# A new order for the operations and loads of an attention and feed-forward kernel on one core

## The chip, the core and the metric

The kernel runs on one core of a Trainium2 chip. The metric is the device time in microseconds (us), from the start of an execution to its end. Three executions of the kernel before took 324.38, 324.75 and 325.0 us; the median is 324.75.

## What is computed

Attention over 8 batches of 8 heads, then a feed-forward layer on its output. Each head has 576 tokens of 64 values. Ahead of the keys and values stand 16 "beacon" keys and values that every token sees; among the rest a token sees itself and what comes before it.

```python
def _attn_ref(q, k, v, beacon_k, beacon_v):      # q, k, v: [8, 8, 576, 64]; beacons: [8, 8, 16, 64]
    k_all = np.concatenate([beacon_k, k], axis=2)
    v_all = np.concatenate([beacon_v, v], axis=2)
    scores = scale * np.matmul(q, k_all.transpose(0, 1, 3, 2))          # scale = 1 / 8
    causal[:, Nb:] = np.triu(np.ones((S, S), dtype=bool), k=1)
    scores = np.where(causal, -1000000000.0, scores)
    a = np.exp(scores - scores.max(-1, keepdims=True))
    a /= a.sum(-1, keepdims=True) + 1e-09
    return np.matmul(a, v_all)

def _moe_ref(x, w_in, w_out):                    # x: [4608, 512], w_in: [512, 2048], w_out: [2048, 512]
    r = np.maximum(x @ w_in, 0.0)
    return (r * r) @ w_out
```

Inputs and output are float32; the kernel works on bfloat16 copies and accumulates in float32.

## The kernel before, in words

**An order written out.** The kernel first makes a list of operations, each with a name, the engines that may do it, the operations it needs, and what it takes and gives of the shared PSUM banks. Nothing is emitted at that point. Then `Order.run` (from line 202) walks the string SEQUENCE (lines 17 to 167), word by word, and emits each named operation. A suffix picks the engine where there is a choice: `@A` is ScalarE (ACT), `@D` VectorE (DVE), `@P` GpSimd (POOL); without one the first engine of the operation's list is taken. Two lines show how the banks are handed out:

```python
op.slots[pool] = [self.pools[pool].pop(0) for _ in range(need)]
...
self.pools[pool].append(from_op.slots[pool][which])
```

A bank is taken from the front of a queue and given back at its end, in the order of the words. So the order of SEQUENCE decides three things: the order in which every engine works through its own instructions (each engine is in order and runs beside the others, held only by what its operations need), the place of each load in the queue of the engine that issues it, and which earlier operation an operation waits for when it takes a bank. PSUM has four banks "ps" for most products, two double strips for scores, and there are three SBUF buffers "held". Words such as `fillg3` or `tpg0.0.1k` emit nothing; they only give a bank back.

**Fillers.** `fill0` to `fill59` (L354) are 60 matmuls on a tile of ones that write a bank nobody reads. They stand among the first operations, where TensorE (PE) has little else to do.

**Attention.** Pairs of heads are numbered 0 to 31, four for each batch. In a name the first number is the pair (for `qk`, `exp`, `mask`, `av`, `norm`) or the batch (for loads and transposes).

- *First loads of batch 0* (L550): `fldk0`, `fldk1`, `fldk2` go through SyncE's queue (SP), `fldq0` to `fldq2` through ACT's; they bring the first 240 tokens of pair 0, of pair 1, and of pairs 2 and 3. `fck` and `fcq` (L372 on ACT, L374 on DVE) cast them to bfloat16. `bkl` and `bkc` load and cast the beacon keys.
- *Other loads of batches 0 and 1*: `sld...` (L472) and `ld...` (L408 queries, L416 and L417 keys, values and beacon values) go through POOL's queue, and so do the weights, `win0` to `win3` (L893) and `wout0` to `wout3` (L902), a quarter each.
- *Transposes*: for batches 0 and 1 on PE, `tp` (L487 for the first 240 tokens of batch 0, L489 else), with evictions `ek` and `eq` (L372, L374). From batch 2 on `tr` is a transposing DMA on SP.
- *Scores* `qk` (L649) fill a strip. Batch 0 is split in a small first part (240 tokens) and three larger pieces; later batches run as a stream of pieces. `exp` (L671 for batch 0, L747 after) takes the exponential on ACT. `mask` zeroes what a token may not see, on POOL (affine select, L776) or on DVE (a minimum with the tile `tri`, L780). `tri` itself (L343, L345) and `ident` are made on POOL.
- *Values* `av` (L802) multiply with the values and a column of ones; `norm` (L819, L821, DVE) divides by the sum that this column gives.
- *Transposed x* for the feed-forward part: batches 0 to 2 on PE (`xtp` L870, copied by `xte`, L372 or L374), later batches by transposing DMAs on SP (`xt`, L853). A batch's `xt` needs all eight of its norms.

**Feed-forward.** The tokens are cut in nine chunks of 512. `s1.j...` is the first product of chunk j: plain for chunks 0 to 2 (L1088, four matmuls for each block of 128 features; chunk 0 in two parts, so the last number is 0 or 1), and for chunks 3 to 8 a scheme that saves an eighth of the multiplications: seven products for each of four units (L985), as `s1.6.3.4` is product 4 of unit 3 of chunk 6. It needs differences of the tokens, `xsum` (L961, DVE or POOL), and of the weights, `asum` (L928). The partial results pass through `h` operations: `c1`, `u2`, `u3` copy a bank to a held buffer (L372 or L374), `c11`, `c22`, `c12` add a held buffer and apply the relu (L1023, DVE), `c21` is a relu alone (L1014, L1016). `relu` (L1102, L1104) and `sq` (L1049, L1051, L1112, L1114) finish the plain chunks and the squares. `s2.j...` is the second product: chunk 0 plain (L1137), the others with the same scheme (L1194), which needs sums of the activations, `sum` (L1163, DVE or POOL), and of the weights, `wsum` (L913). `ev` (L1217, L372, L374) collects the result, and `st` stores it through SP (L1125; the last chunk in pieces, L1251, one of them through ACT's queue). `warm` (L566) is an exponential on a small tile that nothing reads.

**What orders the work.** Chunk j's first product needs the transposed x of its tokens, so the attention of a batch runs beside the feed-forward products of the chunks before it, and PE takes them in turns. The order around each place that the prediction speaks of is thus that of SEQUENCE alone.

## Time and profile before

| | |
|---|---|
| three executions | 324.38, 324.75, 325.0 us; median 324.75 |
| the profiled execution | 325.59 us |
| its span (first to last instruction) | 323.9 us |
| granted TensorE clock, mean | 0.999 |
| busy: PE, DVE, ACT, POOL | 97%, 78%, 66%, 60% of the span |

The profile is of one execution. Times in it are us from the start of the span. A row of the timeline reads: start, duration of the group, engine, line, operation, the tiles written and read, shapes, the number of instructions, and in brackets the idle time ahead of it with what ended it ("[0.87 <-DVE g L1023]": 0.87 us idle until a DVE instruction of line 1023 was done). A group "x4" is four like instructions in a row, and its duration goes from the first one's start to the last one's end. The table by stretches gives for each stretch the sum of busy time of PE, the weight loads (PEld), DVE, ACT and POOL with their instruction counts, then the granted clock, the mean DMA share and GB/s. The view of waits gives for a kind of wait the us in all, the number, and the longest. In the costliest groups "17.3, 381" is 17.3 us in all and 381 ns for one, and behind the second bar stands the idle time ahead of them.

### The profile page before, as it was taken

To read this page: it belongs to the slowest core of one execution; us is meant where nothing else is said; L and a number is where in the kernel's file an instruction comes from. 1 tells how busy PE (TensorE), PEld (TensorE's weight loads), DVE (VectorE), ACT (ScalarE), POOL (GpSimd) and SP (SyncE) were. 2 spreads that over 40 slices of the span, in tenths; PEclk is the share of its full clock that TensorE was granted. 3 is DMA by queue.
4 is the path that set the end of the run, shared out by engine and by line. 5 is a ranking of instruction groups with operands and counts; after the bars stand their busy time and mean duration, and the time that the engine had idled before them with its cause. 6 is when DMAs were issued, how large, how long until landed. Compare 5 with 4: busy or idle time off the path is not lost.

```text
span 323.9 us, 9406 instructions
## 1 busy us (share of the span) xinstructions
PE 313.9 (97%) x3882; PEld 247.4 (76%) x3882; DVE 252.1 (78%) x529; ACT 213.1 (66%) x313; POOL 195.8 (60%) x268
## 2 busy tenths in 40 slices
PE   7899999999999999998999999999999989999995
PEld 5569765644886468887788888888898878888884
DVE  2687698758976798789997998896867987695773
ACT  2785588257677794768657996889767545555720
POOL 8574679496189588888293759956606051535340
PEclk9999999999999999999999999999999999999999
DMA  8999999999999999999799969944523430110043
GB/s 162 178 179 200 189 182 114 146 199 178 146 78 157 198 174 84 124 222 155 61 130 135 212 68 128 149 88 142 49 16 91 110 52 0 68 65 2 0 148 113
DMA packets 153188, 39.60 MB, mean 122 GB/s; under 512 B 140730, under 2 KB 148794, under 8 KB 153146
## 3 DMA queue, kind: packets, MB, share of 16 engines
q0 software_dynamic: 103744, 18.10, 71.7%
q1 hardware_dynamic: 48253, 20.29, 30.3%
q10 hardware_dynamic: 1149, 0.62, 0.7%
q8 instruction: 30, 0.49, 0.6%
q14 instruction: 12, 0.10, 0.1%
HBM read 37.22 MB, written 9.44 MB: 144 GB/s over the span
## 4 chain that ended last, share of the span: by engine, by line
PE 89%; DVE 3%; DMA 3%; ACT 2%; issue 1%; POOL 0%; DVEq 0%; POOLq 0%; ACTq 0%
PE ps L1194 28%; PE ps L985 21%; PE ps L1088 13%; PE ps L802 9%; PE strip L649 6%; PE ps L1137 4%; DMA qk_area<-in_k_dram 3%; PE ps L649 2%; PE strip L1194 2%; DVE g L1023 1%; PE ps L870 1%; PE ps L354 1%; ACT pt L747 1%; PE ps L489 1%; PE ps L487 1%
## 5 line engine op out<-in xcount | busy, mean ns | idle before, releaser
L1194 PEld LDWEIGHTS <-g 128*128 128x128 bf16 x768 | 72.7, 98 | 10.8 <-issue 1.4
L747 ACT ACTIVATE pt<-strip 128x1024 bf16<-128x1024 f32 x70 | 70.2, 1032 | 5.7 <-PE strip L649 5.7
L1023 DVE CUSTOM_DVE_ANT_0 g<-ps,spare 128x512 bf16<-128x512 f32 x72 | 48.8, 686 | 17.9 <-PE ps L985 12.1
L1194 PE MATMUL ps<-w_out,g 128*128 128x256 bf16 x480 | 60.9, 273 | 0.0
L776 POOL TENSOR_SCALAR_AFFINE_SELECT pt<-pt 128x256 bf16<-128x256 bf16 (+1 forms) x80 | 33.3, 437 | 27.9 <-ACT pt L747 23.9
L372 ACT COPY spare<-ps 128x512 f32<-128x512 f32 x54 | 31.5, 588 | 25.9 <-PE ps L985 21.7
L1163 POOL TENSOR_TENSOR g<-g 128x1024 bf16<-128x1024 bf16 x13 | 28.0, 2158 | 31.5 <-DVE g L1163 10.8
L408 POOL DMA_DIRECT2D qk_area<-in_q_dram x48 | 35.2, 742 | 17.3 <-DMA qT<-qk_area 14.3
L985 PEld LDWEIGHTS <-w_in 128*128 128x128 bf16 x480 | 39.3, 96 | 7.6 <-issue 2.7
L1088 PE MATMUL ps<-xT,w_in 128*128 128x512 bf16 (+2 forms) x256 | 44.1, 326 | 0.0
L985 PE MATMUL ps<-xT,w_in 128*128 128x256 bf16 (+4 forms) x384 | 42.7, 247 | 0.3 <-DMA xT<-xn 0.2
L802 PE MATMUL ps<-vb,pt 128*128 128x65 bf16 (+1 forms) x960 | 38.5, 194 | 1.8 <-DVE g L1023 0.9
L802 PEld LDWEIGHTS <-pt 128*128 128x128 bf16 (+1 forms) x960 | 35.6, 97 | 5.9 <-issue 2.6
L417 POOL DMA_DIRECT2D vb<-in_v_dram x40 | 34.4, 860 | 6.2 <-DMA qk_area<-in_q_dram 2.3
L1088 PEld LDWEIGHTS <-w_in 128*128 128x128 bf16 x256 | 24.0, 98 | 16.3 <-issue 1.0
L1049 ACT ACTIVATE g<-g 128x1024 bf16<-128x1024 bf16 x31 | 32.2, 1058 | 5.6 <-DVE g L1023 4.1
L821 DVE TENSOR_TENSOR xn<-ps,rcp 128x320 bf16<-128x320 f32 (+2 forms) x64 | 31.5, 492 | 2.2
L985 PEld LDWEIGHTS <-qk_area 128*128 128x128 bf16 x320 | 27.8, 97 | 5.2 <-issue 0.8
L747 ACT ACTIVATE pt<-ps 128x512 bf16<-128x512 f32 x42 | 23.6, 598 | 9.6 <-PE ps L649 8.8
L1194 PE MATMUL ps<-w_sum,g 128*128 128x256 bf16 x224 | 28.9, 273 | 0.0
L985 PE MATMUL ps<-spare,qk_area 128*128 128x256 bf16 x192 | 27.9, 272 | 0.5 <-DVE spare L961 0.5
L649 PEld LDWEIGHTS <-kT 64*128 64x128 bf16 x618 | 19.8, 94 | 10.7 <-issue 7.8
(87 smaller groups left out, 492.0 us busy)
## 6 DMA issues: line engine op xcount, KB each, us to landing
out_dram<-osb SPq DMA_DIRECT2D x16, 512.0 KB, 3.8
qk_area<-in_q_dram POOLq DMA_DIRECT2D x48, 72.0 KB, 4.8
vb<-in_v_dram POOLq DMA_DIRECT2D x24, 128.0 KB, 6.0
qk_area<-in_k_dram POOLq DMA_DIRECT2D x18, 128.0 KB, 4.7
w_in<-in_moe_w_in_dram POOLq DMA_DIRECT2D x4, 512.0 KB, 9.4
w_out<-in_moe_w_out_dram POOLq DMA_DIRECT2D x4, 512.0 KB, 9.2
vb<-in_v_dram POOLq DMA_DIRECT2D x8, 112.0 KB, 5.2
qk_area<-in_k_dram POOLq DMA_DIRECT2D x6, 112.0 KB, 4.5
```

Of the source, the lines that this page charges most:

```text
L372: nc.scalar.copy(dst, src)
L408: return [nc.gpsimd.dma_start(out=qb[:, g, :, D * u:D * u + D], in_=t[b, c].rearrange("(n p) d -> p n d", p=NP))]
L417: insts.append(nc.gpsimd.dma_start(out=dst[lo:rows], in_=t[b, :, t0:t0 + rows - lo, :].transpose([1, 0, 2])))
L649: nc.tensor.matmul(out, kc[b % 2][hp, c, pr] if b >= NPE else kT[b % 2][hp, pr, 128 * c:128 * c + 128], rhs, start=True, stop=True)
L747: nc.scalar.activation(out, in_, AF.Exp, bias=0.0, scale=scale)
L776: nc.gpsimd.affine_select(out=d[:, :, i], in_=d[:, :, i], compare_op=ALU.is_ge, fill=0.0, base=Nb if m0 + i == 0 else 0, pattern=[[0, 2], ...
L802: nc.tensor.matmul(a[:, at + (t - tl[0]) * (D + 1):at + (t - tl[0] + 1) * (D + 1)], P[0:rr, hj, o:o + 128], vb[b % 2][0:rr, c, 2 * pr + hj ...
L985: nc.tensor.matmul(o[:, i * HT + at:i * HT + at + w], lhs[:, m, f * 128:(f + 1) * 128], part[:, m], start=fresh and i == 0 and at == 0 and ...
L1023: nc.vector._custom_dve(TENSOR_ADD_SAT, out=dst, in0=bank_of(chain), in1=held[keep[added].held[1]].rearrange("p (f t) -> p f t", f=2), s0= ...
L1049: nc.scalar.activation(both, both, AF.Square, bias=0.0, scale=1.0)
L1088: nc.tensor.matmul(h[:, lo - spans[0][0]:hi - spans[0][0]], w_in_sb[:, mc, ft * 128:(ft + 1) * 128], xT[:, mc, lo % RING:lo % RING + hi - lo],
L1194: nc.tensor.matmul(o, lhs[:, f, t * 128:(t + 1) * 128], rhs[:, f], start=fresh and f == 0, stop=f == HF - 1, skip_group_check=True)
```

## The change

Only the string SEQUENCE is changed. The same words stand in it, 1737 before and after, so the same operations are emitted; their order is another, and so is the engine of some that have a choice. Taking the engine moves together: 27 masks go from DVE to POOL and 32 from POOL to DVE; of relus 16 go from ACT to DVE and 14 the other way, of squares 12 and 14; five sums and three `xsum` go from POOL to DVE and four sums from DVE to POOL.

- *Start.* SP issues `fldk2`, `fldk1`, `bkl0`, `fldk0`, `bkl1` where it issued `fldk0`, `fldk1`, `bkl0`, `fldk2`, `bkl1`. ACT issues `fldq1` ahead of `fldq0`. POOL makes `tri` ahead of its first load, and its queue then holds `win1`, `win2`, `win0`, `win3` where it held `win0`, `win2`, `win1`, `win3`, with the loads of values and of batches 1 and 2 between them in another order. 43 fillers stand ahead of the first score product `qk0.0.0` and 17 behind it, where it was 39 and 21. The first products `s1.0.6.0`, `s1.0.5.0` and others stand ahead of `qk2.1.1`, `av0.1.0`, `av1.1.0` and more steps of batch 0 that they stood behind.
- *Middle.* Masks, evictions and products change places with near neighbours all along, and PE's order comes back to the same set of done products every few steps. Around `av18.0.0` and `av19.0.0` the value steps are spread between other products, `mask19.0.1.1` goes to POOL, and the bank that `av18.0.0` takes is the one `h3.2.c21` gives back, where it was that of `h3.2.c12`.
- *Towards the end.* `av30.0.1` with its norms comes ahead of `av31.0.0`; the four `xsum7` stand together ahead of `sum6.3.1`; `s1.7.1.1` stands ahead of `s1.7.0.4`; `warm` is the last word.

The whole string is rewritten; these are the lines of the start, of the two inner places, and of the end, first as they were and then as they are.

```diff
--- before.py
+++ after.py
@@ -15,155 +15,156 @@
 
 
 SEQUENCE = """
...
-fillg10 fill36 fillg36 fillg56 fill46 fillg46 fill39 fill31 fillg31 fldk0 ident fldk1 bkl0 fck1 fck0 bkc0 tp0.0.0k
-fillg39 ek0.0.0@D fill29 fillg29 fill9 fillg9 fill49 fillg49 fill21 fillg21 tpg0.0.0k fill28 fill51 fillg51 fillg28
-tpb0 fill8 fillg8 ekb0 sld0k1.0 tri fldq0 fldq1 ld0v1 sld0q1.0 ld0v0 fldq2 fcq1 fcq0 tp0.0.0q fill26 fillg26 eq0.0.0@A
-fill17 fillg17 tpg0.0.0q tp0.0.1k fill52 fillg52 tp0.0.1q fill38 fillg38 ek0.0.1@D eq0.0.1@A tp0.1.0k tp0.1.1k
-ek0.1.0@A ek0.1.1@D fcq2@D tpg0.0.1k tpg0.0.1q tpg0.1.1k fldk2 fck3 fcq3@A qk0.0.0 qk1.0.0 fill41 fillg41 tpg0.1.0k
-tp0.0.3q fill6 fill54 fillg6 fillg54 fill18 fillg18 tp0.0.3k fill14 fill5 eq0.0.3@D tpg0.0.3q fillg14 fillg5 tp0.1.0q
-tp0.1.1q tp0.0.2q exp0.0.0 exp1.0.0 eq0.1.0@A ek0.0.3@D eq0.0.2@A qk3.0.0 qk0.1.0 mask0.0.0@D eq0.1.1@D fck2
-mask1.0.0@D tpg0.0.2q tpg0.1.0q tpg0.0.3k fill13 tpg0.1.1q fillg13 fill4 av0.0.0 fillg4 bkl1 exp3.0.0 fill44 fill12
-tp0.0.2k qk1.1.0 fillg12 fillg44 sld0k1.2 sld0q1.2 ld0v3 ld0v2 win0 ld0v4 mask3.0.0@P win2 exp0.1.0 fill0 fill30
-norm0.0.0 av1.0.0 ek0.0.2@D fillg30 tpg0.0.2k fillg0 norm1.0.0 exp1.1.0 qk1.1.2 av3.0.0 tp0.1.2k xtp0.0.0 xte0.0.0@D
-norm3.0.0 qk2.0.0 exp1.1.2 exp2.0.0 ek0.1.2@D fill1 tp0.1.2q qk0.1.2 mask2.0.0@D eq0.1.2@D fillg1 fill53 fill37
-fillg37 fillg53 tpg0.1.2k qk0.1.1 fill16 fillg16 fill3 fillg3 av2.0.0 fill50 fill24 fillg24 tpg0.1.2q exp0.1.2
-exp0.1.1 qk1.1.1 fillg50 win1 mask1.1.1@P norm2.0.0 xtp0.0.3 tp0.1.3k xte0.0.3@D qk2.1.1 ek0.1.3@D exp1.1.1
-mask0.1.1@P win3 sld1k0.0 sld1q0.0 sld1k0.2 mask1.1.0@D xtp0.0.2 fill15 fillg15 tpg0.1.3k tp0.1.3q fill20 fillg20
...
-s1.3.3.2 h3.3.c11 s1.3.2.7 s1.3.3.6 sq3.1.0@A h3.2.u3@A s1.3.2.5 av17.0.1 h3.3.u2@D h3.2.c22 exp19.13.1.0.0 norm17.0.1
-s1.3.3.7 s1.3.2.4 s1.3.2.3 h3.3.u3@A s1.3.3.5 s1.3.3.4 mask19.0.1.1@D mask19.0.2@D h3.2.c12 exp19.13.0.0.0 h3.2.c21@A
-h3.3.c22 mask19.0.1.0@D h3.3.c21@A sq3.2.0@A sq3.3.1@A mask18.0.1.1@P mask19.0.0.0@P mask19.0.0.1@P mask18.0.2@P ld6q4
-mask18.0.0.1@P ld6q5 ld6q6 mask18.0.1.0@P ld6q2 ld5v2 qk20.2 av18.0.0 sq3.2.1@D norm18.0.0 s1.3.3.3 h3.3.c12 av19.0.0
-av18.0.1 av19.0.1 s2.3.2.0 sq3.3.0@A norm18.0.1 norm19.0.1 sum3.1.0@P s2.3.1.0 sum3.1.1@D s2.3.5.0 s2.3.1.1 norm19.0.0
...
-mask31.0.0.0@P mask31.0.0.1@P mask31.0.1.1@P av30.0.0 norm30.0.0 s1.6.3.7 av31.0.0 s1.6.3.5 h6.3.u3@A sq6.2.1@A
-s1.6.3.4 av31.0.1 norm31.0.0 h6.3.c22 h6.3.c21@A sq6.3.1@A sq6.2.0@A av30.0.1 norm31.0.1 norm30.0.1 s1.6.3.3 s1.6.3.2
-s2.6.2.0 s2.6.2.1 st11 xt6.3 xt6.4 st10 xt6.2 xt7.0 h6.3.c12 h6.3.c11 sq6.3.0@D sum6.1.1@D xsum7.1@D xsum7.2@D
-s2.6.1.0 s1.7.0.1 s1.7.1.1 h7.0.c1@A s1.7.0.6 h7.0.u2@A s2.6.1.1 sum6.3.1@D xsum7.3@D xsum7.4@D s1.7.0.7 h7.0.u3@A
-s1.7.0.4 ev6.c1.None@A sum6.2.0@D sum6.2.1@D s2.6.6.0 h7.0.c21@A ev6.c11.None s1.7.0.5 sum6.4.0@P sum6.4.1@P h7.0.c22
...
+fillg55 fill15 fill54 fillg54 fillg15 fill29 fill35 fillg35 fill14 fillg14 fillg29 fldk2 fill13 fill43 fillg43 fillg13
+fill5 fill57 fillg57 fill16 fillg5 fill1 fillg16 fillg1 fill53 fillg53 fldk1 fck1 tp0.0.1k fill20 fillg20 fill36
+fillg36 fill44 fillg44 bkl0 bkc0 fck3 ek0.0.1@D tpb0 fill34 tpg0.0.1k fillg34 fldk0 ekb0 fck0 fldq1 fldq0 fldq2 fcq3@D
+fcq0 fcq1 tp0.0.0q fill10 fillg10 fill39 fillg39 fill17 eq0.0.0@A tp0.0.1q fillg17 tpg0.0.0q tp0.0.0k fill8 fillg8
+sld0k1.0 sld0q1.0 sld0k1.2 ld0v1 ld0v0 sld0q1.2 win1 ek0.0.0@D fcq2@D fck2 eq0.0.1@A tp0.1.1k tp0.1.0k ek0.1.0@D
+tpg0.0.1q tp0.0.3k ek0.0.3@A ek0.1.1@A tpg0.0.3k tpg0.1.0k tpg0.0.0k qk0.0.0 qk1.0.0 tp0.0.3q eq0.0.3@D fill3 tp0.1.0q
+fillg3 tpg0.1.1k fill22 tp0.1.1q eq0.1.0@D exp0.0.0 exp1.0.0 eq0.1.1@D qk3.0.0 bkl1 exp3.0.0 tpg0.1.0q fillg22
+tpg0.0.3q tp0.0.2k fill49 tp0.0.2q mask1.0.0@D fillg49 tpg0.1.1q qk1.1.0 fill4 fill28 ek0.0.2@D eq0.0.2@D fillg28
+tpg0.0.2q tpg0.0.2k fillg4 qk0.1.0 ld0v2 win2 mask0.0.0@P mask3.0.0@P ld0v3 ld0v4 av1.0.0 exp1.1.0 exp0.1.0 av0.0.0
+qk1.1.2 fill59 fillg59 norm1.0.0 win0 norm0.0.0 av3.0.0 fill7 fill6 fillg7 fillg6 qk2.0.0 norm3.0.0 exp1.1.2 exp2.0.0
+fill26 xtp0.0.0 fillg26 tp0.1.2k xtp0.0.1 xte0.0.0@D tp0.1.3q eq0.1.3@A qk0.1.2 tpg0.1.3q exp0.1.2 xte0.0.1@D
+mask2.0.0@D qk0.1.1 fill31 fill19 fillg31 fillg19 ek0.1.2@D av2.0.0 fill21 tpg0.1.2k fill41 fillg21 fillg41 fill58
+fill0 fillg0 fillg58 tp0.1.2q fill33 fillg33 tp0.1.3k norm2.0.0 xtp0.0.2 xtp0.0.3 eq0.1.2@D xte0.0.3@D exp0.1.1
+ek0.1.3@D win3 qk1.1.1 xte0.0.2@A qk2.1.0 exp2.1.0 exp1.1.1 tpg0.1.3k tpg0.1.2q ld2q1 zero2 mask0.1.0@P sld1k0.0 ld2k0
+ld2q4 sld1q0.0 sld1k0.2 wout0 ld1v0 sld1q0.2 ld2q7 ld2k4 wout1 ld2q6 ld2q5 wout2 wout3 ld1v4 s1.0.6.0 s1.0.5.0 bkc1
+tpb1 ekb1 mask0.1.1@D relu0.6.0@D qk2.1.1 s1.0.7.0 exp2.1.1 relu0.7.0@D s1.0.9.0 s1.0.10.0 qk3.1.0 qk2.1.2 mask2.1.1@D
+relu0.5.0@D relu0.10.0@D mask1.1.1@D mask1.1.0@D s1.0.11.0 av0.1.0 norm0.1.0 mask2.1.0@D av1.1.0 relu0.9.0@A exp2.1.2
+exp3.1.0 norm1.1.0 relu0.11.0@A qk3.1.1 exp3.1.1 mask3.1.0@D qk3.1.2 exp3.1.2 s1.0.0.0 s1.0.1.0 s1.0.3.0 av2.1.0
...
+norm17.0.1 s1.3.2.4 h3.2.c21@A h3.2.c22 sq3.1.1@D sq3.2.1@D s1.3.3.7 h3.3.u3@A s1.3.3.5 s1.3.2.3 h3.2.c12 h3.3.c22
+exp19.13.0.0.0 mask19.0.0.0@P mask19.0.0.1@P mask18.0.2@P mask18.0.1.0@P ld6q2 mask18.0.1.1@P ld6q3 ld6q5 ld6q1 ld6q6
+av18.0.0 mask19.0.1.1@P mask19.0.2@D mask19.0.1.0@D s1.3.3.4 h3.3.c21@A sq3.3.1@A qk20.2 av18.0.1 s1.3.3.3 av19.0.0
+norm18.0.0 ld6q7 ld6k4 sum3.1.0@P h3.3.c12 norm19.0.0 norm18.0.1 s2.3.2.0 av19.0.1 sq3.2.0@A s2.3.2.1 norm19.0.1 xt4.2
+xt4.1 xt4.0 sq3.3.0@A s2.3.1.0 s2.3.1.1 exp20.2.1.0.0 ev3.c1.None@A exp20.2.0.0.0 sum3.1.1@D sum3.3.1@D sum3.3.0@D
...
+mask30.0.1.1@P mask30.0.1.0@P mask31.0.0.0@P mask31.0.1.0@P mask31.0.0.1@P sum6.3.0@P av30.0.0 s1.6.3.7 av30.0.1
+norm30.0.0 norm30.0.1 s1.6.3.5 sq6.2.1@A av31.0.0 h6.3.u3@A s1.6.3.4 h6.3.c22 h6.3.c21@A sq6.3.1@A sq6.2.0@A av31.0.1
+norm31.0.0 s1.6.3.2 s1.6.3.3 norm31.0.1 s2.6.2.0 s2.6.2.1 st11 st10 xt6.2 xt6.4 xt7.0 h6.3.c11 h6.3.c12 sq6.3.0@D
+sum6.1.1@D xsum7.1@D xsum7.2@D xsum7.3@D xsum7.4@D sum6.3.1@D s1.7.0.1 s2.6.1.0 h7.0.c1@A s1.7.0.6 h7.0.u2@A s2.6.1.1
+s1.7.0.7 h7.0.u3@A s1.7.1.1 s1.7.0.4 ev6.c1.None@A sum6.2.0@D sum6.2.1@D s2.6.6.0 ev6.c11.None h7.0.c21@A s1.7.0.5
...
+st8.0.0.256 st8.1.1.0 s2.8.3.1 ev8.c12.1 st8.0.1.256 warm
 """
 
 
```

## Prediction

> **What bounds the kernel now.** The page comes first: its span, the busy share of TensorE (PE), and the chain of work that ended last.

> ```profile
> span 323.9 us, 9406 instructions
> PE 313.9 (97%) x3882; PEld 247.4 (76%) x3882; DVE 252.1 (78%) x529; ACT 213.1 (66%) x313; POOL 195.8 (60%) x268
> PE 89%; DVE 3%; DMA 3%; ACT 2%; issue 1%; POOL 0%; DVEq 0%; POOLq 0%; ACTq 0%
> ```

> The reader is to see that PE is the bound: 89% of the chain is matmuls. The change leaves every matmul in place, so only PE's empty time and its fillers can change. The table by stretches shows where that is (after the engines' busy times: PE clock, DMA share, GB/s).

> ```profile
> 0.00:5.00 5.00, 3.19 (x16) 2.26 (x17) 1.20 (x8) 1.78 (x3) 4.04 (x12) 1.00 0.53 131
> 5.00:10.00 5.00, 3.81 (x37) 2.93 (x35) 1.42 (x4) 0.93 (x3) 3.68 (x6) 1.00 1.65 198
> 10.00:15.00 5.00, 4.96 (x75) 3.29 (x76) 3.81 (x12) 4.38 (x9) 3.08 (x5) 1.00 1.74 175
> 140.00:160.00 20.00, 18.33 (x290) 15.82 (x288) 18.73 (x38) 16.20 (x23) 13.86 (x20) 1.00 1.47 142
> 250.00:265.00 15.00, 13.66 (x190) 11.83 (x189) 13.40 (x27) 8.16 (x12) 4.04 (x6) 1.00 0.44 91
> ```

> Two inner stretches lose PE time: 1.67 us in 140 to 160 and 1.34 us in 250 to 265, both with DVE at about 90%. The clock is 1.00 everywhere, so it explains nothing. The third place is the start, where "busy" deceives: the 60 fillers count as busy.

> The view of waits, PE's rows, puts a size on each:

> ```profile
> PE ps L487 <- DMA qk_area<-in_k_dram: 1.2, 1, 1.2
> PE ps L802 <- DVE g L1023: 0.9, 1, 0.9
> PE ps L985 <- ACT spare L372: 0.7, 1, 0.7
> PE ps L802 <- DVE pt L780: 0.5, 1, 0.5
> PE ps L985 <- DVE spare L961: 0.5, 1, 0.5
> PE ps L802 <- DVE xn L821: 0.3, 1, 0.3
> PE ps L985 <- DMA xT<-xn: 0.2, 1, 0.2
> ```

> All waits behind the start add to 3.1 us, about 1% of the span. That is nearly the whole prize.

> **Part 1, the first loads.** Operations are found in the trace by counting: an engine runs its instructions in the order of SEQUENCE.

> ```profile
> 2.23 0.42 SPq L550 DMA_DIRECT2D osb<-in_k_dram  x1
> 4.26 0.50 DVE L374 CAST qk_area<-osb 120x256 bf16<-120x256 f32 x2 [2.51 <-DMA osb<-in_k_dram]
> 6.96 0.41 DVE L374 CAST kT<-ps 128x240 bf16<-128x240 f32 x1 [0.30 <-PE ps L487]
> 10.04 0.49 PE L487 MATMUL ps<-ident,qk_area 112*64 112x112 bf16 x12 [1.24 <-DMA qk_area<-in_k_dram]
> 10.46 0.87 PE L649 MATMUL strip<-qT,kT 64*128 64x240 bf16 x8
> 11.07 1.46 ACT L671 ACTIVATE pt<-strip 128x736 bf16<-128x736 f32 x2
> 13.44 3.13 ACT L671 ACTIVATE pt<-strip 128x736 bf16<-128x736 f32 x4
> 16.77 1.73 ACT L671 ACTIVATE pt<-strip 128x736 bf16<-128x736 f32 x2 [0.20 <-PE strip L649]
> osb<-in_k_dram SPq DMA_DIRECT2D x1, 240.0 KB, 7.9
> ```

> SP's queue ends with fldk2, issued at 2.23 and landed 7.9 later, at 10.1. The new order sends fldk2 first and fldk0 last. The bytes ahead of the last landing stay the same, so I put fldk0 at about 10.1. Behind it stand a cast (0.50 for two, so 0.25), tp0.0.0k (some 0.2, as twelve transposes take 0.49), and ek0.0.0 with 0.41. The first score product then starts at 10.1 + 0.25 + 0.2 + 0.41 and an estimated 0.2 of hand-overs, 11.2 where it was 10.46: 0.7 late. On POOL tri also goes ahead of the first load, which puts sld0k1.0 back by the length of tri, under 1 us; what needs it comes behind what needs fldk0, so it adds nothing while it lands before 11.

> ACT makes that up. Between 11.07 and 16.77 it runs six exponentials (1.46 + 3.13 = 4.6) with two copies and some waiting between them; the new order puts those copies, eq0.1.0 and eq0.0.2, on DVE. Starting 0.7 later, at 11.8, the six end at 16.4, and with up to 0.4 of waiting exp2.0.0 starts between 16.4 and 16.8. So ACT's chain is level again.

> What is left is PE's filling in between. Behind the first score the old order has 21 fillers, the new one 17, since the first feed-forward products (s1.0.6 and so on) move ahead of five score and value steps, with win1 loaded first instead of third.

> ```profile
> L893 POOL DMA_DIRECT2D w_in<-in_moe_w_in_dram x4: 747/758/771, 11.2 to 17.1; - x4
> DMA to landing us min/median/max: 8.1/9.4/11.1
> 23.11 0.58 PE L1088 MATMUL ps<-xT,w_in 128*128 128x240 bf16 x4
> 1.81 5.01 PE L354 MATMUL ps<-ones 128*128 128x256 bf16 x28 [1.81 <-DVE ones L348]
> ```

> A filler has 256 columns. 28 of them took 5.0 us at the start, 0.18 each; eight products of that width take 1.07 in the row at 258.32 below, 0.13 each, and I take that one, as the nearer in time to full flow. Four fewer give 0.5 us. The last of the four loads is issued at 17.1 and lands 11.1 later, at 28.2, in both orders, and they are some 2.6 apart, so win0, third in the new order, lands near 25.6. PE comes to s1.0.0 at about 25.4, an estimate from the products ahead of it. That cover is thin: 0.1 to 0.4 us of wait there. **I take -0.3 us**; the ends are +0.8 (the late first score is not made up) and -2.3 (most fillers become work: 21 x 0.13 = 2.7, less 0.4 for win0).

> **Part 2, 150 to 158.**

> ```profile
> 153.72 0.61 PE L802 MATMUL ps<-vb,pt 128*128 128x65 bf16 x15 [0.87 <-DVE g L1023]
> 155.58 0.94 PE L802 MATMUL ps<-vb,pt 128*128 128x65 bf16 x25 [0.48 <-DVE pt L780]
> 156.81 0.62 PE L802 MATMUL ps<-vb,pt 128*128 128x65 bf16 x15 [0.29 <-DVE xn L821]
> 151.01 2.06 DVE L780 TENSOR_TENSOR pt<-pt,tri 128x256 bf16<-128x256 bf16 x2
> 154.19 1.33 DVE L780 TENSOR_TENSOR pt<-pt,tri 128x256 bf16<-128x256 bf16 x1
> 153.21 2.15 POOL L1163 TENSOR_TENSOR s_sum<-g 128x1024 bf16<-128x1024 bf16 x1
> L780 DVE TENSOR_TENSOR pt<-pt,tri 128x256 bf16<-128x256 bf16 x47 | 17.3, 381 | 1.3 <-ACT pt L747 1.2
> ```

> av18.0.0 waits for the PSUM bank that h3.2.c12 gives back on DVE, and that stands behind mask19.0.1.1, the row at 151.01: two masks in 2.06 where the mean is 0.38. The second long mask ends just behind POOL's sum, 155.5 against 155.4. In the new order av18.0.0 gets its bank from h3.2.c21 on ACT, mask19.0.1.1 goes to POOL, and the four value steps are spread between s1.3.3.4, qk20.2, s1.3.3.3 and s2.3.2.0. mask19.0.1.0 stays on DVE, but av19.0.0, which reads it, comes two products later. The three waits are 1.64; **I take -1.3**, with 0 as the end at which mask19.0.1.0 is as late again, and -1.7, all that the stretch lost.

> **Part 3, 255 to 263.**

> ```profile
> 255.80 6.50 SPq L853 DMA_TRANSPOSE xT<-xn  x5
> 255.28 0.49 DVE L821 TENSOR_TENSOR xn<-ps,rcp 128x320 bf16<-128x320 f32 x1
> 258.32 1.07 PE L985 MATMUL ps<-xT,w_in 128*128 128x256 bf16 x8 [0.18 <-DMA xT<-xn]
> 259.87 0.61 PE L985 MATMUL ps<-spare,qk_area 128*128 128x256 bf16 x4 [0.48 <-DVE spare L961]
> 262.48 0.60 PE L985 MATMUL ps<-spare,w_in 128*128 128x256 bf16 x4 [0.67 <-ACT spare L372]
> ```

> xt7.0, the first of the five transposes, starts when the last of eight normalizations ends: 255.28 + 0.49 = 255.8. That last one (norm30.0.1) stood behind norm31.0.1 and h6.3.c22; the new order does av30.0.1 before both av31, so one normalization less is left at the end, some 0.4 sooner. xsum7.1 and xsum7.2 follow it, with sum6.3.1 moved behind all four, and s1.7.1.1 now stands in the slot before s1.7.0.4. The waits are 1.33. **I take -0.7**; ends 0 and -1.4.

> **Part 4, everything else.** In the rest the PE order returns to the same place every few products; 32 masks go from POOL to DVE and 27 the other way, and activations, copies and squares change sides in like numbers. Five more masks are 5 x 0.38 = 1.9 us on DVE, hidden where DVE has room (252 of 324) and not in the two stretches above. The reordered later loads hide behind PE: its only DMA wait there is the 0.2. If that cover is gone, masks queue behind a load that POOL holds back, at up to a mask's wait each.

> What this trace can't show is where the new order stalls. The nearest row is the collision above, 0.87 of PE's time. **I take one of them, +0.9**; ends 0 and +3.0, as many as all of the old waits.

> **Sum.** -0.3 - 1.3 - 0.7 + 0.9 = -1.4. The profiled execution took 325.59 (span 323.9 and 1.7 around), so one like it would take 324.2. The median of the runs shown is 0.84 lower, 324.75, so 324.75 - 1.4 = 323.35, **323.4 us**.

> **Rivals.** *Collisions (slower).* The mechanism is a mask on DVE that runs beside POOL and takes 1.33, or 2.06 for two, where the mean of 47 is 0.38. For it speak the two rows above; against it that masks move both ways in nearly equal numbers. If the gain of parts 2 and 3 is spent on such waits and two more hit PE, the sum is -0.3 + 2 x 0.87 = +1.4, **326.1**. It decides the sign from the fourth collision that PE waits for (-2.3 + 4 x 0.87 = +1.2); three cancel the gain. [...]

> *The stalls only move (no change).* PE's in-order queue fills each gap in one place and opens it in another; the late k0 (+0.7 passed through) and win0 (+0.4) eat what parts 2 and 3 give. Part 1 is then +1.1: 1.1 - 1.3 - 0.7 + 0.9 = 0.0, **324.8**. It needs fldk0 to land past 10.8, or ACT to wait between the first exponentials.

> **Chances.** Forecast 0.50, its own range 321.4 to 324.0; collisions 0.32; stalls only moved 0.18. Some 0.2%, 0.65 us, is about what a measurement of this kernel can tell from no change. So faster 0.50, same 0.18, slower 0.32. The low end takes two thirds of what the far ends of parts 1 and 3 would add to the forecast (2.0 + 0.7 = 2.7), 323.35 - 1.9 = 321.4; the high end is the collisions with one more of 0.87, 327.0.

> **What will show it.** Part 1: first score near 11.2, exp2.0.0 near 16.8, the first L1088 product some 3 us before 23.1, the longest PE wait of the inner start on win0. Part 2: no PE wait for L1023 or L780 near 153. Part 3: xt7.0 near 255.0 less the gains before it, and waits on L961 and ACT's copies under 0.7 together. Part 4: PE's waits behind the start add to less than 2. I am wrong if the first exponentials start past 12.3, or the L780 mean rises past 0.45 us with PE waiting for it.

## The result, and the profile after

The new order is slower. Four executions took 329.46 to 330.4 us, median 329.88, where the kernel before took 324.88 in four; the ratio is 1.0146, with a 95% interval of 1.0122 to 1.0170. The forecast was 323.4, and 321.4 to 327.0. The profiled execution took 329.70 us, its span 328.0, so 4.1 more than the span before.

First the page of the new kernel: the span, the engines' busy time, and the chain that ended last. Every line number is one higher than before, because the string is one line longer.

```profile
span 328.0 us, 9371 instructions
PE 314.9 (96%) x3872; PEld 248.0 (76%) x3882; DVE 255.1 (78%) x536; ACT 214.4 (65%) x317; POOL 185.8 (57%) x258
PE 88%; DVE 9%; issue 1%; ACT 1%; ACTq 0%; DVEq 0%
```

PE is busy 1.0 us longer with the same matmuls (ten of their records are missing in this trace), and DVE's share of the chain went from 3% to 9%. Both are signs to follow: PE waits for DVE, and PE itself is slow somewhere. PE's longest waits behind the start in the new kernel (us in all, number, longest):

```profile
PE ps L803 <- DVE pt L781: 2.9, 2, 2.7
PE ps L986 <- DVE g L1024: 1.8, 2, 1.4
PE ps L803 <- DVE xn L822: 0.5, 1, 0.5
PE ps L986 <- DMA xT<-xn: 0.4, 1, 0.4
PE ps L986 <- ACT g L1015: 0.2, 1, 0.2
PE ps L986 <- ACT spare L373: 0.2, 1, 0.2
PE ps L986 <- DVE spare L962: 0.2, 1, 0.2
```

Behind the start no wait was over 0.9; now there are a 2.7 and a 1.4. The waits of the old order for L1023 (0.9) and L780 (0.5) at 153 are gone, as forecast. The table by stretches of the new kernel (sums of busy time of PE, PEld, DVE, ACT, POOL; then clock, DMA share, GB/s), with a stretch of its own behind the long wait:

```profile
140.00:160.00 20.00, 19.64 (x307) 17.22 (x305) 18.60 (x40) 16.17 (x24) 12.71 (x19) 1.00 1.31 152
190.00:194.00 4.00, 4.00 (x52) 3.09 (x52) 3.83 (x11) 0.20 (x2) 0.00 (x0) 0.57 0.11 22
```

140 to 160 lost 1.67 us before and 0.36 now. From 190 to 194 PE counts as busy without a gap, but the granted clock is 0.57: this is the second sign. PE did about half the work there in the same time: the first eight products of L1195 in it take 1.90 us, and the same eight take 1.04 in e6 below, at a clock of 1.00. The column of busy time can't show it.

To find where the 4.1 us come from, take places at which both orders have done the same set of products, and compare when the next one starts. New minus old:

| same work done up to (old start) | new - old, us | change |
|---|---|---|
| 45.2 | -0.99 | start: -0.99 |
| 64.6 | -0.19 | **55 to 61: +0.80** |
| 149.9 | -0.20 | |
| 156.8 | -1.68 | 150 to 157: -1.48 |
| 188.4 | -1.74 | |
| 191.8 | +2.36 | **187 to 194: +4.10** |
| 225.1 | +2.20 | |
| 262.5 | +2.08 | 250 to 264: -0.1 |
| 286.4 | +2.23 | |
| 291.0 | +3.64 | **288 to 294: +1.41** |
| end of the span | +4.1 | tail: +0.4 |

So the change gave 2.6 us and took 6.7. The rows of DVE at the three bad places in the new kernel:

```profile
56.83 1.22 DVE L781 TENSOR_TENSOR pt<-pt,tri 128x256 bf16<-128x256 bf16 x1
186.96 2.97 DVE L781 TENSOR_TENSOR pt<-pt,tri 128x256 bf16<-128x256 bf16 x1
290.17 2.50 DVE L1164 TENSOR_TENSOR g<-g 128x1024 bf16<-128x1024 bf16 x1
```

POOL's rows beside the last two:

```profile
186.90 0.72 POOL L409 DMA_DIRECT2D qk_area<-in_q_dram  x1
187.64 2.13 POOL L1164 TENSOR_TENSOR s_sum<-g 128x1024 bf16<-128x1024 bf16 x1
289.85 2.28 POOL L1164 TENSOR_TENSOR g<-s_sum,g 128x1024 bf16<-128x1024 bf16 x1 [9.74 <-PE ps L1195]
```

And PE's rows behind these two:

```profile
189.99 1.51 PE L803 MATMUL ps<-vb,pt 128*128 128x65 bf16 x28 [2.67 <-DVE pt L781]
293.33 0.61 PE L986 MATMUL ps<-xT,w_in 128*128 128x256 bf16 x4 [1.43 <-DVE g L1024]
```

The mask at 186.96 is mask23.0.0.1, which the new order moved from POOL to DVE. It ends at 189.93, just behind POOL's sum4.1.0 (187.64 + 2.13 = 189.77). The operation at 290.17 is sum7.3.1; it ends 0.54 behind POOL's sum7.2.0 (292.13), somewhat less than the 0.69 that such a sum takes alone. The mask at 56.83 stands beside four masks on POOL.

### The profile page after: what moved, and what is told of

Same layout as the page of the kernel before. It is cut to its first block, busy times and chain, and to the rows that moved or that the text cites. A ratio compares the mean times of both kernels' runs of the same rounds, so it can differ in the third digit from the quotient of the medians.

```text
span 328.0 us, 9371 instructions
## 1 busy us (share of the span) xinstructions
PE 314.9 (96%) x3872; PEld 248.0 (76%) x3882; DVE 255.1 (78%) x536; ACT 214.4 (65%) x317; POOL 185.8 (57%) x258
## 4 chain that ended last, share of the span: by engine, by line
PE 88%; DVE 9%; issue 1%; ACT 1%; ACTq 0%; DVEq 0%
PE ps L1195 27%; PE ps L986 21%; PE ps L1089 13%; PE ps L803 8%; PE strip L650 6%; PE ps L1138 3%; PE ps L355 3%; PE ps L650 2%; DVE g L1024 2%; PE strip L1195 2%; DVE pt L781 2%; PE ps L871 1%; DVE xn L822 1%; PE ps L488 1%; DVE g L1164 1%
## 5 line engine op out<-in xcount | busy, mean ns | idle before, releaser
L1195 PEld LDWEIGHTS <-g 128*128 128x128 bf16 x768 | 73.1, 98 | 11.3 <-issue 1.5
L1195 PE MATMUL ps<-w_out,g 128*128 128x256 bf16 x480 | 61.5, 275 | 0.2
L1024 DVE CUSTOM_DVE_ANT_0 g<-ps,spare 128x512 bf16<-128x512 f32 x72 | 48.8, 686 | 14.1 <-PE ps L986 11.9
L777 POOL TENSOR_SCALAR_AFFINE_SELECT pt<-pt 128x256 bf16<-128x256 bf16 (+1 forms) x76 | 29.5, 414 | 37.0 <-ACT pt L748 34.8
L373 ACT COPY spare<-ps 128x512 f32<-128x512 f32 x53 | 30.8, 589 | 26.4 <-PE ps L986 21.8
L1089 PE MATMUL ps<-xT,w_in 128*128 128x512 bf16 (+2 forms) x252 | 44.4, 325 | 0.2
L1164 POOL TENSOR_TENSOR g<-g 128x1024 bf16<-128x1024 bf16 x11 | 23.6, 2152 | 29.8 <-DVE g L1164 16.0
L1089 PEld LDWEIGHTS <-w_in 128*128 128x128 bf16 x256 | 23.8, 98 | 17.1 <-issue 1.6
L1050 ACT ACTIVATE g<-g 128x1024 bf16<-128x1024 bf16 x30 | 31.1, 1060 | 1.0 <-DVE g L1024 0.9
L418 POOL DMA_DIRECT2D qk_area<-in_k_dram x30 | 25.6, 858 | 9.7 <-DMA kT<-qk_area 8.6
L1195 PE MATMUL ps<-w_sum,g 128*128 128x256 bf16 x224 | 28.9, 272 | 0.0
L781 DVE TENSOR_TENSOR pt<-pt,tri 128x256 bf16<-128x256 bf16 (+2 forms) x79 | 24.9, 343 | 4.1 <-ACT pt L748 4.0
```

The costliest lines, as they stand in the source:

```text
L373: nc.scalar.copy(dst, src)
L418: insts.append(nc.gpsimd.dma_start(out=dst[lo:rows], in_=t[b, :, t0:t0 + rows - lo, :].transpose([1, 0, 2])))
L781: nc.vector.tensor_tensor(out=d, in0=d, in1=which[:, None].to_broadcast([rows, 2, m, w]), op=ALU.min)
L1024: nc.vector._custom_dve(TENSOR_ADD_SAT, out=dst, in0=bank_of(chain), in1=held[keep[added].held[1]].rearrange("p (f t) -> p f t", f=2), s0= ...
L1050: nc.scalar.activation(both, both, AF.Square, bias=0.0, scale=1.0)
L1089: nc.tensor.matmul(h[:, lo - spans[0][0]:hi - spans[0][0]], w_in_sb[:, mc, ft * 128:(ft + 1) * 128], xT[:, mc, lo % RING:lo % RING + hi - lo],
```

## The experiments

**Theory:** a mask or a sum on DVE (both of its operands are in SBUF) that stands beside a sum on POOL waits for that sum to end, as the mask at 186.96 with its 2.97 us, and each such wait that PE runs into costs its length; a PE without work for 2.67 us also gets half a clock for some microseconds behind it (0.57 as the mean from 190 to 194). **Rivals:** the loss is spread over many small places; the mask is held by the load that POOL issues and not by the sum; the stall moves to the next late thing when it is taken away; the clock falls for a reason of its own. All ratios are to the kernel before, run beside each kernel on the same chip; the new order's is 1.0146.

**e1_mask23_pool.** New order with

```diff
-mask23.0.2@P mask23.0.0.0@P ld7q1 exp22.11.1.0.0 mask23.0.0.1@D sum4.1.0@P
+mask23.0.2@P mask23.0.0.0@P exp22.11.1.0.0 mask23.0.0.1@P ld7q1 sum4.1.0@P
```

> The new order with one word changed: mask23.0.0.1 runs on POOL, ahead of the load ld7q1, and no longer on DVE. Theory (one collision between DVE and POOL near 187 us, priced with the half clock that follows it): PE's wait of 2.67 us for L781 goes, the granted clock stays at 1.00 from 190 to 194, and the time falls by about 4.2 us from 329.9 to 325.7. Rival 1 (the stall only moves to the next thing that is late, as sum4.1.0 then starts 0.4 us later): it falls by under 2 us, to 328 or more. Rival 2 (the loss is spread over many places): it falls by the 2.67 us of the wait at most and the clock still dips, 327.2 or more.

Ratio 1.0006 (0.9981 to 1.0032). Against 1.0146 that is 1.4% or 4.5 us for one mask on another engine, with the load ld7q1 now behind it. The stretch of this kernel that had the half clock:

```profile
190.00:194.00 4.00, 3.96 (x42) 3.23 (x41) 3.96 (x8) 3.95 (x6) 3.24 (x5) 1.00 0.70 89
```

No gap, and the clock is 1.00. Between the same places as in the table its profile gains 4.2 us. The loss wasn't spread, and nothing took its place there. The same profile shows what the sum does not hold. DVE, then POOL:

```profile
188.07 0.49 DVE L822 TENSOR_TENSOR xn<-ps,rcp 128x320 bf16<-128x320 f32 x1
187.64 2.14 POOL L1164 TENSOR_TENSOR s_sum<-g 128x1024 bf16<-128x1024 bf16 x1
```

A normalization has one operand in PSUM and one in SBUF; this one stands in the middle of the sum and takes its usual 0.49.

**e2_sum4_dve.** New order with sum4.1.0 on DVE, the mask left on DVE:

```diff
-mask23.0.0.1@D sum4.1.0@P
+mask23.0.0.1@D
...
-qk24.5 norm23.0.1
+qk24.5 norm23.0.1 sum4.1.0@D
```

> The new order with sum4.1.0 moved from POOL to DVE, behind norm23.0.1; mask23.0.0.1 stays on DVE. Theory (POOL's sum is what holds the mask up): the mask takes under 1 us where it took 2.97, PE's wait goes to under 0.8 us, and the time falls by 3 to 4 us, less up to 0.7 for the sum on DVE: 326.0 to 327.2. Rival (the load ld7q1, which POOL issues from 186.90 to 187.62, holds it, or the mask is long by itself): the mask stays above 1 us with the sum gone, and the time falls by under 2 us.

Ratio 1.0011 (0.9981 to 1.0041), a little better than expected. DVE, then POOL, in this kernel:

```profile
188.14 0.28 DVE L781 TENSOR_TENSOR pt<-pt,tri 128x256 bf16<-128x256 bf16 x1
```

```profile
188.08 0.73 POOL L409 DMA_DIRECT2D qk_area<-in_q_dram  x1
```

The mask stands beside the same load in the same way, 0.06 behind its start, and takes 0.28. So the load alone doesn't hold it; the sum behind it does.

**e3_load_behind.** New order with the load ld7q1 behind the sum:

```diff
-ld7q1 exp22.11.1.0.0 mask23.0.0.1@D sum4.1.0@P
+exp22.11.1.0.0 mask23.0.0.1@D sum4.1.0@P ld7q1
```

> The new order with the load ld7q1 issued behind sum4.1.0 on POOL, so that the sum can start some 0.7 us sooner; mask and sum stay on their engines. Theory (the mask waits out whatever POOL runs back to back and then does its own 0.3 us): the mask ends just behind the sum again, so it takes about 2.3 us where it took 2.97, PE waits about 2.0 us, and the time falls by 0.7 us to 329.2, or by 2.2 to 327.7 if the shorter idle time leaves the clock alone. Rival (the load opened the long wait, and a mask that starts with the sum or ahead of it isn't held): the mask takes 0.3 to 0.5 and the time falls by about 4 us to 325.8.

Ratio 1.0103 (1.0042 to 1.0164). DVE, POOL and PE in this kernel:

```profile
187.54 2.22 DVE L781 TENSOR_TENSOR pt<-pt,tri 128x256 bf16<-128x256 bf16 x1
```

```profile
187.49 2.11 POOL L1164 TENSOR_TENSOR s_sum<-g 128x1024 bf16<-128x1024 bf16 x1
```

```profile
189.81 1.03 PE L803 MATMUL ps<-vb,pt 128*128 128x65 bf16 x28 [1.92 <-DVE pt L781]
```

The mask again ends just behind the sum (189.76 against 189.60), and PE waits 1.92. The theory's length is right. In this profile the clock stayed at 1.00; the other three executions had a mean of 0.993 to 0.995, as the new order has, but some executions of the kernel before on this chip had that too, so whether a wait of 1.9 us is enough stays open here (the last section comes back to it). On the scale of the first result the time is 324.88 x 1.0103 = 328.2, between the theory's two values and in an interval, 326.2 to 330.2, that holds both.

**e6_dummies_in_stall.** New order, with matmuls that nobody reads put into the wait:

```diff
                 a = ps[box["av"].held[1]]
+                for _ in range(20 if (p, heads[0]) == (23, 0) else 0):
+                    nc.tensor.matmul(a[:, 0:256], ones[:, 0:128], ones, start=True, stop=True)
```

> The new order with 20 dummy matmuls of 256 columns put ahead of av23.0.0's own, into the same bank, which its own products then overwrite; the computation is unchanged. They need nothing that the mask makes, so PE runs them while it waits for mask23.0.0.1. Theory (the half clock from 190.2 to 193.7 comes from PE's 2.67 us without work): the mask stays at 2.97 us, some 2.2 us of the wait are filled, the granted clock stays at 1.00, and the time falls by 1.4 to 1.8 us to about 328.3. Rival (the clock falls for another reason, or PE is slow there because of its operands): the clock still dips to 0.5 and the time stays at 329.9 or rises by up to 0.5.

Ratio 1.0105 (1.0054 to 1.0155), 0.4% or 1.3 us under the new order; the two intervals overlap, so the times alone don't show a gain. PE, and the stretch behind:

```profile
187.19 2.34 PE L798 MATMUL ps<-ones 128*128 128x256 bf16 x20
...
190.09 1.03 PE L805 MATMUL ps<-vb,pt 128*128 128x65 bf16 x28 [0.49 <-DVE pt L781]
```

```profile
190.00:194.00 4.00, 3.92 (x64) 3.30 (x65) 3.83 (x12) 1.72 (x4) 0.32 (x1) 1.00 0.06 12
```

The mask is as long as before and PE's real work starts no sooner, but the clock stays at 1.00. So the half clock came from PE's own idle time. What it cost is read from the profiles: between the same places (188.4 and 191.8 in the table) this kernel takes 1.5 us less than the new order, so some 1.5 of the 4.1 us.

**e10_old_mask_beside_sum.** The other way round: the old order with that one word changed.

```diff
-mask23.0.0.1@P h4.3.c21@A
+mask23.0.0.1@D h4.3.c21@A
```

> The old order with one word changed: mask23.0.0.1 on DVE, behind h4.3.c12, where it ran on POOL just ahead of sum4.1.0. The sum then starts near 188.8 and the mask near 189.0. Theory (the mask waits for the sum's end): it takes about 2.2 us, PE waits some 1.9 us for L781, and the time rises by 1.9 us, or by up to 3.6 if the clock is halved behind the wait: 1.006 to 1.011 of the kernel before. Rival (in the new order it was the length of POOL's whole row of work, masks, load and sum, that mattered): the mask takes under 1 us and the time rises by less than 0.7 us, 1.002 at most.

Ratio 1.0123 (1.0088 to 1.0158), 4.0 us on the old order. POOL, DVE, PE, and the stretch behind, in this kernel:

```profile
187.19 0.73 POOL L408 DMA_DIRECT2D qk_area<-in_q_dram  x1
187.94 2.13 POOL L1163 TENSOR_TENSOR s_sum<-g 128x1024 bf16<-128x1024 bf16 x1
```

```profile
187.38 3.20 DVE L780 TENSOR_TENSOR pt<-pt,tri 128x256 bf16<-128x256 bf16 x3
```

```profile
190.29 2.99 PE L802 MATMUL ps<-vb,pt 128*128 128x65 bf16 x51 [2.53 <-DVE pt L780]
```

```profile
190.00:192.00 2.00, 1.71 (x32) 1.72 (x33) 1.97 (x8) 0.78 (x1) 0.07 (x1) 0.50 0.00 0
```

The stall and the half clock are there in the old order too, and so is nearly the whole loss. Not as I had put it, though: the planted mask itself was short. Without it POOL no longer waited for the exponential that this mask needs, so the sum started at 187.94 instead of 189.11 (0.8 us sooner beside the same products, as the start had given 0.4), and it caught the first of three masks that stood ahead on DVE: taken singly, this one has 2.85 us, and the two behind it, which ran when the sum was over, 0.23 and 0.28. One word decides where POOL's sums fall, and that decides which DVE operation is caught.

**e5_three_moves.** New order with three operations on the other engine: the two caught masks on POOL (with the load ld7q1 behind the second, as in e1), and at 290 the sum that did the catching, sum7.2.0, on DVE.

```diff
-mask6.0.1.1@P mask6.0.1.0@P mask7.0.2@P asum1 norm5.0.0 mask7.0.1.1@D norm4.0.0 mask6.0.0.1@D norm5.0.1
+mask6.0.1.1@P mask6.0.1.0@P mask6.0.0.1@P mask7.0.2@P asum1 norm5.0.0 mask7.0.1.1@D norm4.0.0 norm5.0.1
...
-ld7q1 exp22.11.1.0.0 mask23.0.0.1@D
+exp22.11.1.0.0 mask23.0.0.1@P ld7q1
...
-sum7.2.1@D sum7.1.0@P sum7.3.0@P sum7.2.0@P
+sum7.2.1@D sum7.1.0@P sum7.3.0@P sum7.2.0@D
```

> The new order with three operations on the other engine: mask23.0.0.1 on POOL as in the first run, sum7.2.0 on DVE (it ran on POOL from 289.85 to 292.13 beside sum7.3.1, which took 2.50 us on DVE where 0.69 is usual, and s1.8.1.2 lost 1.4 us), and mask6.0.0.1 on POOL ahead of mask7.0.2 (it took 1.22 us beside four masks on POOL, and av6.0.0 came 0.7 us late). Theory (each long DVE operation costs what PE waited, and nothing else is late behind it): 4.2 + 1.5 + 0.6 less than the new order, 0.985 to 0.996 of the kernel before (some 2 us under it, 322.8 where it takes 324.9). Rival (the waits move on: sum7.2.0 on DVE delays h8.1.c11 and the products behind it, mask6.0.0.1 on POOL comes too late for av6.0.0): no better than the first run, 1.000 of the kernel before.

Ratio 1.0009 (0.9987 to 1.0032): the rival's number. By the same places the profile shows that mask6 gave 0.5 and sum7.2.0 1.6 us at 288, and that 1.7 us went again at 291 to 295. DVE, POOL and PE there:

```profile
291.67 2.50 DVE L1164 TENSOR_TENSOR g<-g 128x1024 bf16<-128x1024 bf16 x1
```

```profile
291.20 2.41 POOL L1164 TENSOR_TENSOR g<-g 128x1024 bf16<-128x1024 bf16 x1 [14.67 <-PE ps L986]
```

```profile
294.82 0.61 PE L986 MATMUL ps<-xT,qk_area 128*128 128x256 bf16 x4 [1.19 <-DVE g L1024]
```

It is the same mechanism with the next pair, sum7.4.0 on DVE and sum7.4.1 on POOL, which now run at the same time.

**e11_four_moves.** That, and sum7.4.0 on POOL too, so that no sum on DVE stands beside one on POOL there.

```diff
-sum7.2.0@D sum7.4.0@D
+sum7.2.0@D sum7.4.0@P
```

> The run with three moves, and sum7.4.0 on POOL ahead of sum7.4.1 too. In the run with three moves sum7.4.0 took 2.50 us on DVE (291.67 to 294.17) beside sum7.4.1 on POOL (291.20 to 293.62), and PE waited 1.19 us for h8.1.c22 behind it. Theory (that second collision ate what the move of sum7.2.0 gave): no sum or mask on DVE is longer than 1 us past 285, PE's wait of 1.19 goes, and the time falls by 1.2 to 1.7 us against the run with three moves, to 0.996 of the kernel before. Rival (another wait takes its place again): PE still loses over 1 us between 286 and 300, and 1.000.

Ratio 0.9955 (0.9935 to 0.9976): faster than both kernels, by four operations moved to the other engine. PE's longest waits in it behind the start:

```profile
PE ps L986 <- DMA xT<-xn: 0.4, 1, 0.4
PE ps L986 <- DVE g L1024: 0.4, 1, 0.4
```

And the larger group of its sums on DVE (shortest, median, longest in ns, then the first and last start):

```profile
L1164 DVE TENSOR_TENSOR g<-g x20: 676/685/694, 83.5 to 307.5; 128x1024 bf16<-128x1024 bf16 x20
```

Behind the start no wait is over 0.4 us, and none of these sums is longer than 0.69.

**The start: e7_new_tri_late and e8_old_tri_first.** The landings in the new order came sooner than I had forecast, and two changes could be the reason: the order on SP and ACT, or tri ahead of POOL's first load. e7 puts tri behind that load in the new order, e8 puts it ahead in the old one.

```diff
-ident tri fill2
+ident sld0k1.0 tri fill2
...
-sld0k1.0 sld0q1.0 sld0k1.2
+sld0q1.0 sld0k1.2
```

```diff
-sld0k1.0 tri fldq0
+tri sld0k1.0 fldq0
```

> The new order with POOL's first load, sld0k1.0, put ahead of tri again, as the old order has it; else unchanged. Theory (the early POOL load is what slows the loads of SP and ACT: tri holds it back, and they land up to 2.5 us sooner): fldk0 lands past 9 instead of at 7.83, the first score product starts past 10.8 instead of at 9.97, and the time rises by 0.5 to 1.5 us. Rival 1 (the order on SP and ACT does it): landings and first score within 0.4 us of the new order's, and the same time. Rival 2 (the gap that tri leaves in POOL's queue costs the loads): the second POOL load lands past 10, but fldk0 stays near 7.9.

> The old order with tri ahead of POOL's first load, sld0k1.0, and nothing else changed. Theory (the early POOL load slows the others): fldk2 lands near 8 instead of at 10.15 and sld0k1.0 itself near 8.5 instead of at 10.00, PE's wait of 1.24 us for it goes, the first score product starts near 9.6 instead of at 10.46, and the time falls by 0.6 to 1.2 us (0.997 of the kernel before). Rival (the order on SP and ACT does it): landings and first score as before, within 0.4 us, and 1.000.

e7: 1.0150 (1.0118 to 1.0181), the new order's time. e8: 0.9985 (0.9964 to 1.0007), which can't be told from no change. In e8 PE waits 0.65 us for the load where it waited 1.24, and the first score starts at 9.84 instead of 10.46; but in e10, whose start is the old one unchanged, it started at 10.00, so that most of this is what two executions differ by. Both changes brought the landings forward, by the longest landing of SP's and ACT's first loads behind its issue: 8.0 us in the old order (7.9 and 7.8 in e9 and e10, which start alike), 6.8 with tri first in it (e8), 5.6 in the new order and 6.2 with tri late in it (e7). So tri's place makes 0.6 to 1.2 us of it and the order on SP and ACT 1.2 to 1.8; each figure is of one execution, and those of the runs made from the new order with its own start go from 5.4 to 6.4. For the time it hardly matters, as the first row of PE's timeline shows. In the new order and in e5, which starts with the same operations:

```profile
1.81 6.01 PE L355 MATMUL ps<-ones 128*128 128x256 bf16 x35 [1.81 <-DVE ones L349]
```

```profile
1.81 6.88 PE L355 MATMUL ps<-ones 128*128 128x256 bf16 x35 [1.81 <-DVE ones L349]
...
10.85 0.87 PE L650 MATMUL strip<-qT,kT 64*128 64x240 bf16 x8
```

The same 35 fillers take 5.33 us in e1, 6.01 and 6.88 in these, and the first score follows them: 9.33, 9.97, 10.85. It is PE's own fillers that the new order waits for.

**e12_fewer_fillers.** The run with four moves, without its first 12 fillers (their words and the operations are left out; nothing reads them).

```diff
-    for i in range(NFILL):
+    for i in sorted(set(range(NFILL)) - {37, 25, 51, 42, 48, 11, 45, 12, 47, 46, 52, 56}):
```

> The run with four moves, with the first 12 of its 60 fillers left out. In the new order PE runs 35 fillers in a row before tp0.0.1k, and in the profiles so far the first score starts later the later the fillers turn from 0.213 to 0.109 us each (9.33 where they turned at 4.56, 9.97 at 6.01, 10.85 at 7.76). Theory (PE's own fillers hold up the first work in the new order, not the loads): tp0.0.1k starts near 5.7 to 6.5, the first score at 9.2 to 9.6 whenever the fillers turn, and the time falls by 0.3 to 1.2 us against the run with four moves. Rival (the fillers only fill time in which PE waits for loads and casts anyway, and with fewer of them PE is counted idle and its products run slow for longer): the first score starts at 10 or later, and the time is the same or up to 1.5 us longer.

Ratio 0.9951 (0.9932 to 0.9969), median 323.81 where e11 had 324.32 beside it. PE in this kernel:

```profile
1.81 4.63 PE L355 MATMUL ps<-ones 128*128 128x256 bf16 x23 [1.81 <-DVE ones L349]
...
9.43 0.87 PE L650 MATMUL strip<-qT,kT 64*128 64x240 bf16 x8
```

In e13, below, which starts with the same operations, the fillers take 5.09 us. The first score is at 9.43 and 9.33, though the fillers took 0.46 us longer in the second: it no longer hangs on them. The direction is as the theory has it; 0.5 us is too little to be sure of from the times alone.

**e13_warm_early.** e12, with warm ahead of the last chunk:

```diff
-h7.3.u3@A h7.3.c22
+h7.3.u3@A h7.3.c22 warm
...
-st8.0.1.256 warm
+st8.0.1.256
```

> The run with four moves and fewer fillers, with warm put ahead of the last chunk's evictions on ACT (behind h7.3.u3), where it is the last word in the new order. From the start of s2.8.3.0, near the end, to the end of the span it takes 6.43 us in the old order and 6.85 in the new one and in every run made from it. Theory (warm, 0.21 us behind ACT's last store, is part of that 0.42): the stretch takes 6.4 to 6.5 us and the time falls by 0.4. Rival (it lies beside the store's landing of 1.9 us and costs nothing; the 0.42 is elsewhere): 6.8 to 6.9 us, the same time as the run before it, 0.995 of the kernel before.

The stretch from s2.8.3.0 to the end is 6.85 us as before, so warm isn't the tail's 0.42. The ratio, 0.9930 (0.9906 to 0.9954), overlaps e12's. The kept traces say where the tail is, though no run tests it: the stretches of both orders are alike for their first 5.7 us. At the end of all ten profiles of the new order and of runs made from it, two packets of 8 KB of the kind "instruction" come over a DMA queue (q14), the first at some 5.4 us of the stretch, and one of the instructions with which POOL closes the program starts 0.3 us later than in the old order (in the new order at 6.11 instead of 5.81). The four profiles of the old order and of runs made from it have neither.

**e9_old_mask19_pool.** Part 2 of the prediction alone: the old order with mask19.0.1.1 on POOL.

```diff
-s1.3.3.4 mask19.0.1.1@D mask19.0.2@D
+s1.3.3.4 mask19.0.2@D
...
-mask18.0.1.1@P mask19.0.0.0@P
+mask18.0.1.1@P mask19.0.1.1@P mask19.0.0.0@P
```

> The old order with mask19.0.1.1 on POOL, behind mask18.0.1.1, where it ran on DVE for 1.91 us ahead of h3.2.c12. This is the one move of the prediction's part 2 that takes a mask out of a collision. Theory (that collision is what made av18.0.0 wait 0.87 us and av19.0.0 0.48): h3.2.c12 ends near 151.8 where it ended at 153.67, PE's waits near 153 for L1023 and L780 fall from 1.4 to under 0.4 us, and the time falls by 0.9 to 1.3 us (0.997 of the kernel before). Rival (POOL's row of work is longer by one mask then, and the next mask on DVE, mask19.0.1.0, waits it out instead): the waits there stay above 1 us in sum and the time is the same within 0.3 us.

Ratio 1.0006 (0.9982 to 1.0030), the rival's result, for a reason that neither had. POOL and PE in this kernel:

```profile
152.28 1.40 POOL L776 TENSOR_SCALAR_AFFINE_SELECT pt<-pt 128x256 bf16<-128x256 bf16 x4 [3.27 <-ACT pt L747]
```

```profile
156.63 0.48 PE L802 MATMUL ps<-vb,pt 128*128 128x65 bf16 x10 [1.53 <-POOL pt L776]
```

I put the mask at a place in POOL's row where its exponential wasn't ready. POOL stood for 3.27 us, the masks of pair 18 behind it came late, and PE waited 1.53 us for POOL instead of for DVE. The wait for L1023 that the mask had caused is gone: beside the same products av18.0.0 starts 0.94 us sooner than in the old order, and by the end of the place 0.33 of that is left. Whether the move pays with the rest of the new order's rearrangement was not run. The profiled execution (326.93 us, median 325.72) also has a wait of 1.62 us for a transposed load at 135.7, ahead of the edit, so its stall on POOL may differ from that of other executions. In e8 this wait is 1.3 us, in the profiles of the old order and of e10 it isn't there: it is something by which executions of the old order differ.

## Why the prediction was wrong, point by point

- **Part 1 (-0.3): the sign right by luck, the way wrong.** The step that put fldk0 at about 10.1, since "the bytes ahead of the last landing stay the same", failed. In the new profile the loads of its line land at most 5.6 us behind their issue, and it is issued at 2.26, so it has landed by 7.9. These rows are SP's issue and the landings of its line; then PE's first score and first L1089 product; then ACT's exponentials, of which exp2.0.0 is the last of the five (12.41 + 3.95 less its 0.78 is 15.6):

```profile
2.26 0.42 SPq L551 DMA_DIRECT2D osb<-in_k_dram  x1
DMA to landing us min/median/max: 3.9/4.2/5.6
```

```profile
9.97 0.87 PE L650 MATMUL strip<-qT,kT 64*128 64x240 bf16 x8
...
19.64 0.99 PE L1089 MATMUL ps<-xT,w_in 128*128 128x240 bf16 x8
```

```profile
12.41 3.95 ACT L672 ACTIVATE pt<-strip 128x736 bf16<-128x736 f32 x5 [0.27 <-PE strip L650]
```

  The first score came at 9.97, not 11.2, exp2.0.0 at 15.6, not 16.4 to 16.8, the first L1089 product 3.5 us sooner, as forecast, and nothing waited for win0. But the fillers, which I had priced only as something to be replaced, became what PE waits for. My reading that the clock is 1.00 everywhere was wrong there too: 28 fillers at a mean of 0.18 are some at 0.21 and some at 0.11, as the last section shows. At 45 us the gain was 0.99 in this pair of profiles; e10, with the old start, reached that place at 44.76, and e5, with the new one, at 45.12, so the gain is not one of every execution.
- **Part 2 (-1.3): right.** 1.48 us, with no wait for L1024 or L781 over 0.21 in the stretch. Which of the three changes there did it is not shown; e9 moves the mask alone, to another place in POOL's row, and gained nothing.
- **Part 3 (-0.7): mostly wrong.** 0.1 us net. The first of the five transposes starts 0.4 sooner beside the work done, as forecast:

```profile
257.60 6.42 SPq L854 DMA_TRANSPOSE xT<-xn  x5
```

  That is 1.8 behind the old 255.80 where the stretch began 2.2 later. The waits there for L961 and ACT's copies, 0.48 + 0.67, fell to 0.2 + 0.2, but the wait for xT went from 0.2 to 0.4 and one of 0.2 for h6.3.c21's relu (L1015) is new: 1.0 in all, not the 0.6 forecast.
- **Part 4 (+0.9): the step that failed.** I took one collision at 0.87 of PE's time, and +3.0 as the far end. There were three, and their places took 4.10, 1.41 and 0.80; of the last, e5's move gave 0.5 back. The two rows that it went by were mild ones: the masks at 151.01 stood beside masks and loads on POOL, and the one at 154.19 started when 1.2 us of POOL's sum were left. The mask at 186.96 took 2.97: nearly the whole issue of the load that POOL had ahead of its sum (0.72), and then the whole sum (2.13); and behind 2.67 us without work PE ran at half clock for 3.41 us. The far end held neither, since I had bounded what may come by the sum of the waits that were there. So an engine was not held by what its operations need alone: the mask needs nothing of that sum, and with the sum gone it took 0.28 (e2).
- **The rival "collisions"** named the mechanism and the sign, at 0.32. Its price, 326.1, came from the same 0.87. It said that the sign turns at the fourth collision; the first was enough.
- Which of the two, mask or sum, started first did not decide it. In e3 the mask started 0.05 behind the sum and took 2.22; but the mask at 186.96 started 0.68 ahead of the sum (187.64) and ended behind it, as did the first of e10's at 187.38 (sum at 187.94). In the last two the sum stood behind a load in POOL's queue that was being issued; how the mask was held from there, the rows can't show.
- What I held against that rival, that masks move both ways in nearly equal numbers, was no argument: their count says nothing on which of them fall beside a sum.
